# Squares on GpSimd in a fused attention and MoE kernel: 36 squares moved, 153 half-size sets, other last blocks

## The chip, the cores and the metric

The kernel runs on one core of one Trainium2 chip. The metric is the device time of one execution in microseconds. The engines are named as in the profile: PE (TensorE), DVE (VectorE), ACT (ScalarE), POOL (GpSimd) and SP (SyncE), which here only issues DMAs. POOL, SP and ACT issue DMAs.

## The reference

```python
# q, k, v: (4, 6080, 256); w_in: (256, 2048); w_out: (2048, 256)
qn = q / (norm(q, axis=1) + 1e-6)
kn = k / (norm(k, axis=1) + 1e-6)
s = kn.transpose(0, 2, 1) @ qn / tau            # (4, 256, 256)
a = exp(s - s.max(-1)); a /= a.sum(-1) + 1e-9
x = (v @ a).reshape(24320, 256)
out = gelu_tanh(x @ w_in) @ w_out
```

The norms run over the 6080 tokens, so that each batch needs the sums of squares of all columns of q and k, and the 256x256 product of k and q (the gram), before its attention matrix exists.

## The kernel before

**Folding.** The attention matrix is multiplied into w_in once per batch. This gives AW (256x2048), and the first layer is then v @ AW. The tokens of a batch are cut into blocks: five of 1024 and one of 960; in the last batch five of 1024, one of 512 and one of 448. A block's two halves, t=0 and t=1, have hc tokens each (512, 480, 256 or 224). There are 25 blocks, numbered 0 to 24.

**First layer of a block.** The 2048 hidden columns are 16 chunks of 128. A chunk and a half is done in one of two ways.
- Plainly: `mm1_one` (j, line 571) does two matmuls, `gelu_one` (J, line 583) one GELU on ACT. In the last blocks both halves can share one matmul (t=2).
- In a set ("half-size set", steps `s`): two chunks times two halves, so four plain products of two matmuls each, are made with seven matmuls of hc columns (`small`, line 639) in place of eight. The set uses sums of weights (`sums_w`, lines 605 to 611) and of v (`sums_v`, lines 618 to 622) that DVE makes. It needs two copies on ACT (cq at line 654, y5 at line 657), two additions on DVE (ap at line 659, ax at line 662) and four GELUs on ACT (lines 664 to 673). A block has at most 8 sets.

**Second layer.** Seven products with combined weights of w_out (`product`, line 750) stand for eight. DVE makes their inputs from the GELU outputs (`sums_g`, steps T, lines 723 to 733: both inputs in SBUF, up to 2048 elements a row). The results are added, transposed on DVE (`turn`, line 779) and stored in four DMAs for each half (`store`, line 795).

**Attention of the later batches.** While the blocks of one batch run, the next batch is prepared: 12 chunks of q and of k are loaded by casting DMAs that POOL issues (`load_one`, lines 254 and 256), PE adds each to the gram (`gram_row`, line 304), and `square_later` (lines 274 and 276) squares it. Step z is a square on ACT, d on DVE and e on POOL (the program before has no step e). A full chunk's square has 1024 elements a row, of bf16, in SBUF. `fold` (lines 284 to 296) adds up the squares on DVE; its first step, f.1, reads the whole chunk's squares of q and k. There are two buffers of squares. Of the 24 squares of each of the three later batches, ACT does 18 and DVE 6 (k of the even chunks).

**First batch.** Its q and k are loaded, squared and summed ahead of everything else. Then `scores` makes the attention matrix and `first_aw` the first 512 columns of AW, scaled by the row sums. `pe_vt` transposes the first block's v on PE.

**Order.** Each engine runs its instructions in the order of one long written list, `ORDER`: one word for a step, with block or batch ahead of the colon (`14:s5cq`, `b3:zq8`, `13:M3A`). Waits between engines follow from the data and the buffers. A DMA load is held back until the matmul has run that stands before it in the list (`GATE`). PSUM has eight banks, which are handed out in the order of the list.

Of the kernel before, what the change touches and what calls it, by code (L numbers as in the profile page):

```python
# [18 lines left out]
def kernel(  # L19
# [23 lines left out]
    HALF = 512  # L43
    SIZES = [[1024] * 5 + [960]] * (B - 1) + [[1024] * 5 + [512, 448]]
# [737 lines left out]
    def store(m, tj):  # L782
# [42 lines left out]
    with tc.manual_schedule():  # L825
# [49 lines left out]
        square_rows(c, 1, 0, 5, "dve")  # L875
# [3 lines left out]
        ss_rows(c, 1, range(0, 5))  # L879
# [105 lines left out]
0:j51 0:J21 0:jb1 0:s7m6 0:ja1 0:Jb1 0:s6ap 0:J51 0:J91 :pF0 0:Ja1 1:j00 0:s7ap :pS3 b0:w02 1:lt1
1:J00 0:s6m3 0:s7m3 0:s6m7 1:j50 0:s6ax 1:J50 0:j01 0:s7G1 b1:r0.0 :pS1 :pF1 0:jb0 0:j61 0:j11
0:s6G1 b1:r0.1 1:j10 0:Jb0 b1:lq1 0:s7m7 b1:lk1 b1:lq2 0:s6Gx 0:s7ax 0:s6m4 0:M1A 0:J01 1:j30 4:lv0
0:s7m4 0:J11 b1:r0.2 8:lv0 b1:lk2 0:T3a b1:lk3 3:lv0 0:M1B 0:s6Gr b1:lq4 0:J61 1:j11 1:J10 1:vs0
0:s7Gr 1:j41 :pA12 0:x1 1:J11 1:j01 1:j51 0:M2A 0:s7Gx 1:j31 1:J51 0:T1a 1:vs1 b1:r0.3 1:J30 1:s3m1
0:M2B b1:dk0 :pS2 1:J41 1:J31 1:j21 b1:zq1 1:s3m5 1:s3y5 0:T3b 1:J01 0:M5A b1:r1.0 0:T2a 1:J21  # L990
b1:r1.1 1:vs2 b1:lk5 0:T1b 1:s3cq b1:zk1 0:c11 0:M6A b1:r1.2 b1:r1.3 1:s3m2 1:s4m1 1:s4cq 0:T2b
2:lv1 b1:lq3 1:s3m6 b1:zq0 0:M5B :pS4 0:M6B 1:s4m6 0:y5 b1:r2.0 1:s4m2 1:s3ap b0:w03 1:s3G0 b1:r2.1
:pNA 0:ap 1:s4m5 1:s3m3 1:s3m7 b1:f1.1 b1:r2.2 1:s3ax b1:lk4 1:s4G0 0:M3A 1:s3G1 0:M3B b1:f0.1 2:lv0
1:s4y5 1:s5m1 1:s3Gx b1:zk3 1:s3m4 0:M7A 2:lt0 1:s4ap 1:s5cq 0:c12 1:s4m3 0:T4a 1:s4m7 1:s6m1 1:s5m2
1:s3Gr 1:s4G1 b1:r2.3 1:s4ax b1:dk2 b1:lq5 b1:f1.2 1:s5G0 1:s5m5 1:s5y5 1:s5m6 1:j20 1:s4m4 0:M7B
1:s5ap 1:s6cq 1:s4Gr 1:s4Gx 1:s6m2 1:s6G0 b1:r3.0 1:s6m5 1:s6m6 1:s5m7 1:s5m3 0:ax 1:j40 2:lt1 1:J20
1:s5G1 0:M4A 0:T4b b1:r3.1 1:J40 1:s6y5 0:M4B b1:f1.3 b1:zq2 1:s5ax 1:s7m5 1:s6ap b1:r3.2 1:s7m1
1:s5Gx b1:r3.3 1:s6m3 1:s7y5 0:c21 1:s5m4 1:s6m7 1:M1A 1:s7cq 1:s7m6 1:s5Gr b1:f2.1 1:M1B 1:T3a
1:s6ax 1:s6m4 1:s7m2 b1:r4.0 1:s6G1 b1:r4.1 1:s7ap 1:s7m3 1:T1a 1:s7m7 b1:zq3 1:s6Gx 1:x1 b1:lk6
1:s6Gr b1:lq6 1:s7ax 2:j30 1:s7G0 b1:lq7 b1:r4.2 1:s7G1 2:j11 1:s7m4 2:j01 1:T2a 1:s7Gx 1:s7Gr  # L1000
b1:f3.1 2:j20 2:vs0 2:vs1 1:M2A 2:J30 2:J20 1:T3b 2:s2m1 3:lv1 1:M2B 2:J11 2:s2m5 1:c11 2:s2cq 1:M6A
# [313 lines left out]
```

## Time and profile before

| | |
|---|---|
| median of 3 runs | 683.74 us (683.71 to 683.79) |
| the profiled execution | 683.82 us |
| its span on the core | 682.1 us, granted clock 0.998 |
| instructions | 10254 |
| HBM read and written | 78.91 MB and 36.57 MB |

A run of the kernel takes 1.7 us more than the span that the profile shows. The page has a line for each part: the busy time of each engine, the span in 40 slices, the queues, the chain of waits that ended last, and the groups of instructions. In a group's line stand the source line, the engine, the operation, output and inputs, the shape, the count, the busy time in us, the mean of one in ns, and the idle time before it with its releaser. Instructions of an engine overlap, so that the time from one start to the next is shorter than the duration of one.

### The profile page before, as it was taken

How to read it: one execution, taken by the hardware profiler on the slowest of the kernel's cores; microseconds unless marked ns; L12 is line 12 of the kernel's file. 1: busy time of each engine (PE TensorE's matmuls, PEld its weight loads, DVE VectorE, ACT ScalarE, POOL GpSimd, SP SyncE). 2: the span in 40 equal slices, each digit the busy share in tenths (PEclk: the TensorE clock that was granted, in tenths of full speed). 3: DMA queues.
4: the chain of work that ended last, by engine and by line, in shares of the span. 5: the costliest groups of instructions: out<-in, count | busy, mean ns of one | idle time of the engine just before them, and what ended most of it. 6: DMA issues, size and time to landing. Idle time of an engine off the chain costs nothing.

```text
span 682.1 us, 10254 instructions
## 1 busy us (share of the span) xinstructions
PE 660.3 (97%) x3412; PEld 333.9 (49%) x3472; DVE 630.5 (92%) x935; ACT 640.7 (94%) x1241; POOL 90.1 (13%) x165
## 2 busy tenths in 40 slices
PE   3999999999999999999999999999999999999996
PEld 2844444544445454454444544454444444444465
DVE  3579999999999999999999999999999999999996
ACT  5389999999999999999999999999999999999983
POOL 4323112111100122101020201200000000000002
PEclk9999999999999999999999999999999999999999
DMA  9997868878545896646884477668343446262453
GB/s 241 208 254 134 148 116 140 144 124 147 109 81 105 130 170 112 116 91 116 137 142 78 82 133 137 100 117 132 61 80 62 78 68 118 43 86 46 76 100 60
DMA packets 164678, 78.80 MB, mean 116 GB/s; under 512 B 148545, under 2 KB 153025, under 8 KB 163905
## 3 DMA queue, kind: packets, MB, share of 16 engines
q0 software_dynamic: 18064, 39.84, 32.9%
q1 hardware_dynamic: 145552, 37.09, 30.3%
q10 hardware_dynamic: 1008, 1.22, 0.6%
q8 instruction: 27, 0.44, 0.3%
q14 instruction: 27, 0.21, 0.1%
HBM read 78.91 MB, written 36.57 MB: 169 GB/s over the span
## 4 chain that ended last, share of the span: by engine, by line
PE 79%; ACT 14%; DMA 4%; issue 2%; POOL 0%; DVE 0%; POOLq 0%; DVEq 0%; ACTq 0%
PE u L750 20%; PE rb L639 15%; PE j L571 11%; PE p L750 10%; PE qb L639 7%; PE c L750 5%; PE G L304 4%; DMA qk<-in_k_dram 4%; PE qa L639 3%; ACT qa L654 2%; ACT g L583 2%; PE awp L512 2%; ACT g L664 2%; ACT yw L657 2%; ACT g L673 2%
## 5 line engine op out<-in xcount | busy, mean ns | idle before, releaser
L750 PEld LDWEIGHTS <-wcomb 128*128 128x128 bf16 x1400 | 136.9, 98 | 143.4
L750 PE MATMUL u<-t,wcomb 128*128 128x512 bf16 (+3 forms) x590 | 144.1, 368 | 0.4
L583 ACT ACTIVATE g<-j 128x512 bf16<-128x512 f32 (+1 forms) x196 | 119.0, 664 | 2.0 <-PE j L571 2.0
L571 PE MATMUL j<-vT,aw 128*128 128x512 bf16 (+2 forms) x410 | 114.6, 376 | 1.0 <-ACT aw L406 0.3
L659 DVE TENSOR_TENSOR qb<-rb,yw 128x512 f32<-128x512 f32 (+3 forms) x142 | 95.7, 676 | 9.2 <-PE rb L639 4.1
L639 PE MATMUL rb<-tv,sw 128*128 128x512 bf16 (+3 forms) x276 | 99.8, 372 | 0.4
L662 DVE TENSOR_TENSOR xw<-rb,yw 128x512 f32<-128x512 f32 (+3 forms) x142 | 94.5, 667 | 6.1 <-PE rb L639 3.1
L750 PE MATMUL p<-g,wcomb 128*128 128x512 bf16 (+3 forms) x393 | 96.4, 368 | 0.4
L673 ACT ACTIVATE g<-xw 128x512 bf16<-128x512 f32 (+3 forms) x142 | 94.3, 666 | 0.0
L670 ACT ACTIVATE g<-rb 128x512 bf16<-128x512 f32 (+3 forms) x142 | 88.7, 636 | 2.6 <-PE rb L639 2.5
L654 ACT ACTIVATE qa<-rb 128x512 f32<-128x512 f32 (+3 forms) x142 | 89.3, 633 | 1.4 <-PE rb L639 0.5
L667 ACT ACTIVATE g<-qb 128x512 bf16<-128x512 f32 (+3 forms) x142 | 88.7, 630 | 1.9 <-PE qb L639 1.5
L657 ACT ACTIVATE yw<-qb 128x512 f32<-128x512 f32 (+3 forms) x142 | 89.1, 632 | 1.5 <-PE qb L639 1.0
L664 ACT ACTIVATE g<-qa 128x512 bf16<-128x512 f32 (+3 forms) x142 | 88.7, 631 | 0.3 <-PE qa L639 0.2
L639 PEld LDWEIGHTS <-sw 128*128 128x128 bf16 x568 | 55.3, 98 | 58.2 <-issue 1.2
L571 PEld LDWEIGHTS <-aw 128*128 128x128 bf16 x428 | 41.6, 98 | 44.0 <-issue 1.5
L639 PEld LDWEIGHTS <-aw 128*128 128x128 bf16 x426 | 41.7, 98 | 42.4 <-issue 0.4
L317 POOL DMA_DIRECT2D vb<-in_v_dram x47 | 23.5, 501 | 276.9 <-PE qb L639 123.0
L729 DVE TENSOR_TENSOR t<-g,g 128x2048 bf16<-128x2048 bf16 (+3 forms) x50 | 58.0, 1162 | 0.3
L731 DVE TENSOR_TENSOR t<-g,g 128x2048 bf16<-128x2048 bf16 (+3 forms) x50 | 58.2, 1163 | 0.1
L723 DVE TENSOR_TENSOR g<-g 128x2048 bf16<-128x2048 bf16 (+3 forms) x50 | 58.1, 1162 | 0.2
L733 DVE TENSOR_TENSOR t<-t,g 128x2048 bf16<-128x2048 bf16 (+3 forms) x50 | 57.7, 1160 | 0.0
(133 smaller groups left out, 1002.7 us busy)
## 6 DMA issues: line engine op xcount, KB each, us to landing
out_dram<-ot SPq DMA_DIRECT2D x160, 128.0 KB, 3.0
vb<-in_v_dram POOLq DMA_DIRECT2D x37, 256.0 KB, 5.1
q<-in_q_dram POOLq DMA_DIRECT2D x33, 256.0 KB, 5.4
k<-in_k_dram POOLq DMA_DIRECT2D x33, 256.0 KB, 5.8
out_dram<-ot SPq DMA_DIRECT2D x24, 120.0 KB, 2.7
wst<-in_moe_w_out_dram POOLq DMA_DIRECT2D x2, 1024.0 KB, 11.2
qk<-in_q_dram POOLq DMA_DIRECT2D x3, 512.0 KB, 14.3
qk<-in_k_dram POOLq DMA_DIRECT2D x3, 512.0 KB, 17.0
```

Of the source, the lines that this page charges most:

```text
L571: GATE[0] = nc.tensor.matmul(hp[:, :n].rearrange("p (t x) -> p t x", t=2) if t == 2 else hp[:, :n], lhsT=AW[b][:, cc, fc * 128 : fc * 128 ...
L583: nc.scalar.activation(g[:, t, fc % 8, :hc], hp[:, :hc], AF.Gelu_apprx_tanh)
L639: GATE[0] = nc.tensor.matmul(acc[:, :hc], lhsT=lhs, rhs=rhs, start=i in (1, 5), stop=True, skip_group_check=True)
L654: nc.scalar.activation(Q0[m, p][:, :hc], RB[m, p][:, :hc], AF.Copy)
L657: nc.scalar.activation(YW[m, p][:, :hc], Q1[m, p][:, :hc], AF.Copy)
L659: nc.vector.tensor_add(Q1[m, p][:, :hc], RB[m, p][:, :hc], YW[m, p][:, :hc])
L662: nc.vector.tensor_add(XW[m, p][:, :hc], RB[m, p][:, :hc], YW.pop((m, p))[:, :hc])
L664: nc.scalar.activation(g[:, 0, e, :hc], Q0.pop((m, p))[:, :hc], AF.Gelu_apprx_tanh)
L667: nc.scalar.activation(g[:, 1, e, :hc], Q1.pop((m, p))[:, :hc], AF.Gelu_apprx_tanh)
L670: nc.scalar.activation(g[:, 0, e + 1, :hc], RB.pop((m, p))[:, :hc], AF.Gelu_apprx_tanh)
L673: nc.scalar.activation(g[:, 1, e + 1, :hc], XW.pop((m, p))[:, :hc], AF.Gelu_apprx_tanh)
L750: GATE[0] = nc.tensor.matmul(ACCS[m, acc][:, :hc], lhsT=wcomb[:, w, fc, :], rhs=x[:, fc, :], start=first and k_ == 0, stop=k_ == 3, skip_g ...
```

## The change

- All d steps and half of the z steps of the later batches become e: POOL squares k of the even chunks and q of the odd ones, 12 in a batch and 36 in all. ACT keeps the other 36.
- The list has 153 sets in place of 142. Blocks 5, 6, 7, 9, 10, 12, 13, 14, 16, 17, 18, 21 and 23 have one more, block 24 none in place of two.
- The last two blocks are of 704 and 256 tokens in place of 512 and 448. Block 23 now does its plain products by halves, block 24 all of its 16 chunks for both halves in one matmul each.
- The last block's stores are issued by ACT and SP alone. Before, its first four were issued by SP, POOL, ACT, POOL.
- First batch: half of k's squares of the last chunk's first piece goes to ACT, and two rows of them are folded on DVE, so that six matmuls sum that piece in place of eight. The first v transposes use two PSUM tiles, and DVE does both copies. The scaling of AW is done in pieces of 128 columns, two on ACT and six on DVE, and the load of the GELU table stands between them, no longer ahead.
- `ORDER` is a new list throughout.

```diff
-    SIZES = [[1024] * 5 + [960]] * (B - 1) + [[1024] * 5 + [512, 448]]
+    SIZES = [[1024] * 5 + [960]] * (B - 1) + [[1024, 1024, 1024, 1024, 1024, 704, 256]]
...
+    def fold_pair(c):
+        o = SQ0[c][:, 0:2, 256:512]
+        nc.vector.tensor_add(o, o, SQ0[c][:, 2:4, 256:512])
...
+    def pe_vt_first():
+        for cc in range(2):
+            VPS[0, 0, cc] = ps = take(("vps", 0, 0, cc), 1, [128, HALF], f"vt_ps0_0{cc}", BF16)[0]
+            for s in range(HALF // 128):
+                nc.tensor.transpose(ps[:, s * 128 : s * 128 + 128], V0[0, 0][:, s, cc * 128 : cc * 128 + 128], ident_bf)
...
-        if (m, t, cc) == (0, 0, 1):
-            nc.scalar.copy(vt(m)[:, t, cc, :], VPS[m, t][:, cc, :])
-        else:
-            nc.vector.tensor_copy(vt(m)[:, t, cc, :], VPS[m, t][:, cc, :])
+        nc.vector.tensor_copy(vt(m)[:, t, cc, :], VPS[m, t][:, cc, :])
...
-        for u in range(2):
+        for u in range(4):
             for ic in range(2):
-                nc.vector.tensor_scalar_mul(AW[b][:, ic, u * 128 : u * 128 + 128],
-                                            ps[0][ic][:, u * 128 : u * 128 + 128], rs[:, ic : ic + 1])
-        for ic in range(2):
-            nc.scalar.activation(AW[b][:, ic, 256:512], ps[1][ic], AF.Copy, scale=rs[:, ic : ic + 1])
+                o, x = AW[b][:, ic, u * 128 : u * 128 + 128], ps[u // 2][ic][:, u % 2 * 128 : u % 2 * 128 + 128]
+                if u < 2 and ic:
+                    nc.scalar.activation(o, x, AF.Copy, scale=rs[:, ic : ic + 1])
+                else:
+                    nc.vector.tensor_scalar_mul(o, x, rs[:, ic : ic + 1])
+            if u == 1:
+                nc.scalar.preload_act_table(AF.Gelu_apprx_tanh)
...
-            if m == LAST and not LAST_OUT:
-                eng = (nc.sync, nc.gpsimd, nc.scalar, nc.gpsimd)[bi]
-            elif m == LAST:
+            if m == LAST:
                 eng = (nc.scalar, nc.sync)[bi % 2]
...
-        square_rows(c, 1, 0, 5, "dve")
+        square_rows(c, 1, 0, 3, "dve")
+        square_rows(c, 1, 3, 5, "act")
+        fold_pair(c)
...
-15:s2y5 15:J10 14:T3b 15:s2m2 17:lv0 15:j11 15:j00 15:s2ap b3:r8.2 15:j20 14:T1b 15:vs2 15:s2G0
-b3:r8.3 15:J00 15:s3m1 15:J11 18:lv1 15:s2m7 14:M5A b3:f7.3 15:s2m3 14:M5B b3:r9.0 15:J20 15:s3cq
...
+13:c22 14:s3Gx 14:s5cq b3:eq7 b3:r7.0 14:s4m3 14:s5y5 b3:ek8 14:s3m4 14:s4m7 14:s5m2 14:s5m6 14:s4ax
+14:s4G1 b3:r7.1 14:s6m1 13:M4A b3:f5.4 14:s5ap 14:s5G0 b3:f7.1 14:s3Gr 14:s6cq 14:s6m5 14:s4Gx
```

More of the change, by code (lines that the diff above doesn't have):

```diff
@@ L339, with pe_vt_first_copy @@
     VPS = {}
+    def pe_vt_first():
[3 more added lines that the diff above has]
+                nc.tensor.transpose(ps[:, s * 128 : s * 128 + 128], V0[0, 0][:, s, cc * 128 : cc * 128 + 128], ident_bf)
+    def pe_vt_first_copy():
+        for cc in range(2):
+            nc.vector.tensor_copy(vt(0)[:, 0, cc, :], VPS[0, 0, cc])
+            give(("vps", 0, 0, cc))
     def pe_vt(m, t):
@@ L878 @@
         ss_rows(c, 0, range(0, 4))
-        ss_rows(c, 1, range(0, 5))
+        ss_rows(c, 1, (0, 1, 4))
         square_rows(c, 1, 5, 8, "dve")
@@ L898 @@
         warm(6)
-        pe_vt(0, 0)
+        pe_vt_first()
         scores()
-        pe_vt_copy(0, 0, 0)
-        pe_vt_copy(0, 0, 1)
-        nc.scalar.preload_act_table(AF.Gelu_apprx_tanh)
+        pe_vt_first_copy()
         first_aw()
@@ L985 @@
[L985 to L1001, printed above, removed]
@@ new lines @@
+b1:lk2 0:vs1 b0:w13 0:J81 0:vs2 0:ja0 0:s7m2 0:s6m5 0:J21 0:Ja0 0:s6m2 0:s6m6 0:j70 0:s6y5 0:J70
+0:s7m5 0:s6G0 b0:w03 0:j41 0:s7G0 b0:w12 0:j51 0:s7y5 0:s7m6 :pF0 0:j60 0:jb1 0:s6ap :pF1 0:J41
+0:s6m7 0:Jb1 0:j11 0:s7ap 1:j30 0:s6m3 0:J60 1:lt1 0:J11 0:J51 b1:r0.0 :pS3 0:s7m3 0:M1A 0:s6ax
+0:s7G1 :pA12 :pS2 0:j31 0:s6G1 1:j20 1:J20 0:M1B 0:J31 1:j10 0:s6Gx b1:r0.1 :pS1 0:T3a 1:J10 b1:lq1
+0:s6m4 0:j71 0:s7m7 1:J30 0:s7ax 1:j50 b1:lk1 1:j11 0:s6Gr 1:j41 2:lv0 0:J71 0:T1a 0:T2a 0:s7m4
+b1:lq2 1:vs0 :pS4 b1:r0.2 1:J50 1:j51 1:vs1 0:x1 b1:lq3 0:s7Gr 1:J11 1:s3m1 1:J41 4:lv0 b1:r0.3
@@ new lines @@
+2:s5m6 b1:r5.3 2:s5y5 2:s5ap 2:s6m1 2:s5G0 2:s4G1 1:M4A 2:s6cq 2:s4ax 2:s4Gx 2:s6m5 1:c22 2:s6y5
+2:s5m3 2:s5m7 1:O1 2:s6m2 2:s6m6 2:s5ax 1:M4B 2:s4m4 2:s6G0 2:s5m4 2:s5G1 b1:ek6 3:j00 b1:r6.0
+b1:r6.1 2:s7m5 2:s5Gx 2:s6ap 1:c21 2:s6m3 2:s6m7 2:s5Gr 2:s7m1 2:M1A 3:J00 2:s4Gr b1:f5.2 b1:eq7
+b1:f7.1 2:s7cq 3:j30 2:s7y5 2:s7m6 2:T3a 2:s6G1 3:J30 2:M1B 2:s6ax b1:lq8 2:s7m2 2:s6Gx 2:s6m4
+2:s7ap b1:r6.2 2:s7m7 2:s7G0 b1:lk8 2:T1a 2:s7m3 b1:r6.3 3:j11 2:s6Gr 3:j31 b1:lk11 2:s7ax b1:lq9
+3:s2m1 2:T2a b1:r7.0 2:s7G1 2:x1 b1:f5.3 2:s7m4 2:s7Gx 2:s7Gr 3:s3m1 b1:r7.1 b1:lk9 3:s3cq 3:vs0
@@ new lines @@
+4:s5m1 4:s3ax b2:lq2 4:s4m6 b1:f11.2 3:T4a 4:J20 4:s4y5 4:s4ap 3:M3B 4:s3m4 4:s5cq 4:s5m6 4:s5m2
+4:s4G0 3:c12 4:s3Gx 4:s5m5 4:s4m3 b1:f11.3 4:s4m7 b2:lk2 4:s5G0 3:M7A 4:s5y5 4:s4ax 4:s4G1 4:s3Gr
+4:s5ap 4:j11 4:s6m5 4:s6m1 4:s4Gx 4:s6cq 4:s5m3 3:M7B 4:s5m7 4:s6m6 4:s6m2 4:J11 b1:f11.4 b1:ss
+3:T4b 4:s5ax 3:ax 4:s5G1 b1:sv b1:pow 4:s6y5 4:j31 4:s5Gx 4:s4m4 4:s6ap 4:s6G0 4:s7m1 3:c22 4:s5m4
+4:J31 5:j10 4:s4Gr 4:T3a 4:s6m7 4:s5Gr 4:s7cq 3:M4A 6:lt0 3:M4B 4:s7m2 4:s7m5 b1:kf 5:J10 2:O1 b1:kr
+4:s7m6 4:s6m3 b1:krp 4:s6ax 4:T1a 4:s7G0 4:M1A 4:s7y5 b1:S0 b1:S1 4:s6Gx b1:th0 5:j31 4:s6G1 b1:th1
@@ new lines @@
+8:s4m2 8:s2Gr 8:s4y5 8:s3ax b2:f5.4 8:s4ap b2:r7.0 7:M5A 8:s3m4 8:s3G1 b2:zq6 7:M5B 8:s3Gx 8:s3Gr
+8:s4m7 7:T2b 7:y5 8:s4m3 8:s5m1 b2:r7.1 b2:lq9 b2:f6.1 b2:lk9 8:s4G1 8:s4ax 12:lv1 8:s5cq 7:M6B
+8:s4G0 8:s5m5 b2:r7.2 b2:f7.2 8:s5y5 7:ap 8:s5m6 8:s5m2 8:s6m1 8:s4m4 7:M3A b2:f7.3 8:s5ap 8:s5m3
+8:s4Gx 8:s4Gr b2:r7.3 8:s5G0 11:lv0 7:T4b 8:s7m5 8:s5G1 8:s5m7 7:M3B 8:s6cq b3:lq2 8:s6m6 8:s6m5
+b2:f7.4 b2:zq8 b2:lq10 8:s5ax b2:ek8 8:s6m2 8:s5m4 b2:r8.0 b2:lk11 7:c12 b2:r8.1 b2:eq9 8:s7m1
+8:s6y5 7:M7A 8:s5Gx 8:s5Gr 8:s6ap 8:s6m7 7:M7B 8:T3a 8:s7cq 8:s6ax 8:s7m2 8:s6G0 8:s7m6 8:s6m3
@@ new lines @@
+8:M4B b2:f11.3 9:s7y5 b2:r10.1 9:s7m6 9:s7m2 b2:r10.2 b2:r10.3 9:s7ap 9:s5Gr b2:f11.4 9:s6Gx 9:s6m4
+10:j01 b3:lk2 9:s7G0 8:c21 11:lv1 9:s7m7 9:s7ax 9:j10 b2:ss 10:s2m1 9:s7m4 b2:r11.0 9:s6Gr b2:r11.1
+10:J01 11:lt1 9:J10 10:s2cq 9:s7m3 9:T3a b2:r11.2 b2:r11.3 9:s7Gx 10:j10 b3:lk0 10:s1m1 10:vs0 b2:sv
+9:s7G1 10:s2m5 9:s7Gr 10:J10 10:vs1 10:s2m6 10:j00 9:T3b 10:s1m5 b2:pow 9:M1A 10:s2y5 b2:gc 10:s2m2
+10:s2ap 8:O0 10:J00 10:s1cq 9:M1B 10:s1m2 10:s2G0 10:vs2 10:s2m3 9:x1 10:s2m7 9:T1b 10:s3m1 10:s1y5
@@ new lines @@
+14:s7ax b3:lk11 14:s7m4 15:j30 b3:r9.1 15:J01 b3:f7.4 14:s7G1 b3:f8.1 15:s2m1 b3:r9.2 14:T2a 14:M2A
+14:s7Gx b3:ek10 15:vs0 15:s2cq 14:s7Gr b3:r9.3 b3:f9.1 15:s2m2 15:vs1 15:j11 15:J10 15:s2m6 15:J30
+15:J11 15:s2m5 b3:eq11 15:vs2 b3:f9.2 15:s2y5 15:s2G0 14:M2B 14:T3b 15:s2ap b3:r10.0 15:j20 b3:r10.1
+b3:r10.2 15:s3m1 15:s2m3 17:lt0 15:s2m7 15:s3m5 14:T1b b3:zq10 15:J20 15:s3cq 14:M6A b3:r10.3
+15:s3y5 15:s2ax 14:c11 15:s2m4 15:s3m6 b3:f9.3 15:s2G1 15:s3ap 15:s3m2 14:M5A 15:s3m7 15:s2Gx
+15:s4m1 15:s3G0 15:s3m3 b3:f9.4 15:s3ax 15:s2Gr 15:s4m5 14:T2b 15:s3G1 b3:r11.0 14:M5B 15:s4cq
@@ new lines @@
+b3:r11.1 b3:r11.2 15:s3Gx b3:r11.3 15:s4m6 14:T4a 15:s4y5 15:s3m4 14:M6B 14:y5 15:s4ap 15:s4m2
+15:s5m5 b3:gc 15:s5m1 15:s4m7 14:ap 15:s3Gr 15:s4G0 b3:zk11 13:O0 15:s6m1 14:M3A 12:O0 15:s5cq
+b3:f10.1 15:s4m3 15:s4ax 15:s4G1 14:T4b 14:M3B 15:s5y5 15:s5m6 15:s4m4 15:s6cq b3:f11.1 15:s4Gr
+15:s5ap 15:s5m2 16:lt1 14:M7A 15:s6m6 15:s5G0 15:s4Gx b3:f11.2 15:s6m5 14:c12 15:s5m7 15:s7m1
+15:s5m3 14:M7B 15:s6y5 15:s7cq 15:s5ax 15:s6m2 15:s5G1 15:s6ap 15:s5m4 15:s5Gx 14:ax 15:s7m2 15:s7m5
+15:s6m7 b3:f11.3 15:s6ax 15:s6m3 15:s7m6 14:M4A 15:s6G0 15:s7y5 15:s7G0 15:s5Gr b3:f11.4 15:s6Gx
@@ new lines @@
+14:M4B 15:s6G1 16:s1m1 15:s6m4 15:s7ap 15:s7m7 15:s7m3 15:T3a 15:s7ax b3:ss 19:lv0 16:s1cq 16:s2m1
+15:s6Gr 14:c21 15:s7G1 15:s7m4 b3:sv 16:s1m2 15:M1A 16:vs0 15:s7Gx 16:s1m5 16:s2cq 16:s2m2 16:s2m5
+16:s1G0 16:s1y5 16:vs1 16:s2y5 16:s2G0 16:s2m6 15:T1a 16:s1m6 16:s1ap 15:M1B 16:j00 16:s1m3 b3:pow
+16:s1m7 15:s7Gr 16:s2ap 16:s2m3 16:s2m7 15:x1 15:M2A b3:kf 16:s1ax 16:s1G1 16:vs2 b3:kr 16:s3m1
+16:s1Gx 16:s1m4 15:M2B 16:s1Gr 16:J00 17:lt1 16:j10 15:T3b 16:s2G1 b3:krp 16:s2ax 16:s3cq 16:s2m4
+15:T1b b3:S0 16:s2Gr 15:M5A 16:s3m2 b3:S1 16:s4m5 16:s4m1 14:O0 15:T2a 16:J10 16:s3m6 15:T2b 16:s3G0
@@ new lines @@
+23:s6m1 23:s6m5 23:s5G0 23:s4m4 23:s5m7 23:s4Gx 22:M7A 23:s6cq 23:s6m6 23:s5m3 23:s4Gr 23:s6y5
+23:s7m1 23:s5ax 23:s5Gx 23:s5G1 23:s6m2 23:s6ap 23:s6G0 23:s7cq 22:M7B 23:s3Gx 23:s5m4 23:T3a
+23:s7m5 23:s7y5 22:ax 23:s6m3 23:s5Gr 23:s7m6 23:s7ap 23:T1a 22:M3B 23:s6m7 23:s7m2 23:s7m7 23:s7m3
+23:s6ax 22:M4A 23:s2Gx 23:s6G1 23:s7ax 23:M1A 22:M4B 23:M1B 24:j22 23:s6m4 21:O1 23:s7G1 23:s7G0
+23:M5A 23:s6Gx 23:s7Gx 24:J22 23:T2a 23:x1 23:T3b 23:T1b 24:j62 22:c22 23:M5B 23:s7m4 23:M6A 24:J62
+23:T2b 23:M6B 22:c12 23:s6Gr 21:O0 24:j02 23:y5 22:c21 24:j12 23:ap 23:s7Gr 24:J02 24:ja2 24:Ja2
@@ new lines @@
+22:O1 23:T4a 23:T4b 24:j32 24:jb2 24:Jb2 23:M7A 22:O0 23:M7B 24:J12 23:M3A 23:M3B 24:j92 24:jd2
+23:ax 24:J32 23:c22 24:j52 24:j72 23:c12 24:j82 24:J92 24:Jd2 24:j42 24:je2 24:jc2 24:J52 24:J82
+24:M1A 24:jf2 24:J72 24:Je2 24:T3a 23:M2A 24:J42 24:Jc2 24:T1a 23:M4A 24:M1B 24:M5A 24:Jf2 24:T2a
+24:T3b 24:T1b 23:M4B 24:x1 24:M6A 24:T2b 24:M6B 23:c21 24:T4b 24:M5B 24:T4a 23:M2B 23:O1 24:y6
+24:M7A 23:c11 24:y5 24:M7B 24:M3A 24:M3B 24:ax 24:M2A 24:M4A 24:a12 23:O0 24:c22 24:M2B 24:c12 24:O1
+24:M4B 24:c11 24:c21 24:O0
```

529 lines of the change are left out of this document (246 added, 283 removed).

## The prediction

> **What bounds the kernel now.** I read the page first, then the busy time by stretch, then the timeline for the pace of each engine, then the groups by shape. The page's first part and its chain:
>
> ```profile
> PE 660.3 (97%) x3412; PEld 333.9 (49%) x3472; DVE 630.5 (92%) x935; ACT 640.7 (94%) x1241; POOL 90.1 (13%) x165
> ...
> PE 79%; ACT 14%; DMA 4%; issue 2%; POOL 0%; DVE 0%; POOLq 0%; DVEq 0%; ACTq 0%
> ```
>
> Three engines are nearly full and POOL is nearly empty. The chain is mostly matmuls, so a matmul saved is worth its pace as long as ACT and DVE keep up. How much DVE has left is read where the later batches' squares run (L274, L276 and the folds that read them), in three stretches; the columns are window, length, then busy PE, PEld, DVE, ACT, POOL:
>
> ```profile
> 68.00:166.00 98.00, 97.48 (x487) 48.37 (x495) 96.47 (x144) 98.00 (x186) 17.33 (x32) 1.00 0.78 136
> 200.00:310.00 110.00, 109.42 (x554) 55.10 (x564) 106.47 (x154) 109.04 (x205) 16.59 (x29) 1.00 0.67 119
> 360.00:470.00 110.00, 109.29 (x551) 54.62 (x560) 106.35 (x154) 109.64 (x207) 12.61 (x24) 1.00 0.63 109
> ```
>
> DVE idles 1.5 + 3.5 + 3.6 = 8.7 us in all of them. That is the whole cushion for anything that slows DVE there.
>
> Busy times overlap, so costs go by start to start, taken from the timeline:
>
> ```profile
> 301.57 0.38 PE L639 MATMUL qb<-tv,sw 128*128 128x512 bf16 x1
> 301.79 0.38 PE L639 MATMUL qb<-vT,sw 128*128 128x512 bf16 x1
> ```
>
> A 512-column matmul costs 0.216, 480 columns 0.202, 448 0.189, 256 0.109, 224 0.096, 128 0.056 (medians of this spacing); 352 columns are taken in proportion, 0.149. The same reading gives ACT 0.477 for a 512 GELU or copy to SBUF, 0.515 for the copy into qa, 0.520 for the GELU from SBUF, and 0.946 for a square of 1024; DVE 0.60 for ap or ax and 0.594 for a square of 1024.
>
> **The sets.** A full-size set swaps four j products (8 matmuls, 4 GELUs) for 7 matmuls, 6 ACT and 2 DVE instructions: PE -0.216, ACT +1.04, DVE +1.20 us. With the new last blocks counted by shape: j matmuls -92x0.216 -16x0.202 -24x0.189 +16x0.149 +32x0.109 = -21.8; set matmuls +70x0.216 +14x0.202 +42x0.149 -35x0.109 -14x0.096 = +19.1; two ss matmuls fewer, -0.2; the second layer's products have the same columns in all. PE: -2.9 us. On ACT the GELUs of j give -23.7 and the sets +36.6. On DVE the sets give +15.0.
>
> **The squares.**
>
> ```profile
> L274 ACT ACTIVATE sq<-q 128x1024 bf16<-128x1024 bf16 x33 | 37.5, 1144 | 0.0
> ...
> L276 DVE TENSOR_TENSOR sq<-k 128x1024 bf16<-128x1024 bf16 x18 | 12.2, 680 | 0.0
> ```
>
> ACT loses 15 squares of 1024, 3 of 768 (0.73) and 3 of 64x256 (0.31): -17.3. DVE loses 18: -10.7. So ACT ends at -4.4, DVE at +4.7 with its small edits (+0.9 for copies, scalings and the fold of the last chunk, -0.5 for the last block's sums of v). By these counts alone DVE would fit: 630.5 + 4.7 stays below PE.
>
> POOL gains the 36. No row shows a large elementwise POOL instruction. The nearest are the two that make the identity:
>
> ```profile
> 4.66 0.27 POOL masks.py:197 MEMSET ident<- 128x128 f32 x1
> 5.00 0.29 POOL masks.py:199 TENSOR_SCALAR_AFFINE_SELECT ident<-ident 128x128 f32<-128x128 f32 x1
> ```
>
> Taking 0.10 of each as fixed (the memsets of one element last 0.10 to 0.12), 128 elements cost 0.17 to 0.19, so 1024 cost 1.5 to 1.64; if nothing is fixed, 2.3. I take 1.64, the instruction that also reads, and keep 1.5 and 2.3. POOL then has 90 + 59 = 149 us of work in 682: it is not the bound. Queued behind a square on POOL are the casting loads of q, k and v. They mostly wait for a matmul anyway (vb idles 123.0 us on qb, 105.0 on rb), so up to 1.6 us of delay is hidden by that pacing; without it, one late transposed v block costs PE up to 1.6. The GpSimd Engine Reference of the Trainium skill (Performance versus the Vector engine) gives about 2.6 cycles an element at 1.2 GHz for two inputs; an estimate by it is 2.2 us a square, which would bring the forecast's sum to about 706; no row here shows it.
>
> **What a POOL square does to DVE** decides the sign. POOL read SBUF during DVE work three times here, in the pow of L439. The longest:
>
> ```profile
> 305.92 1.21 DVE L723 TENSOR_TENSOR g<-g 128x2048 bf16<-128x2048 bf16 x1
> 306.09 1.93 POOL L439 TENSOR_TENSOR rt<-sv,halves 128x4 f32<-128x4 f32 x1 [15.45 <-DVE sv L433]
> 307.05 1.22 DVE L731 TENSOR_TENSOR t<-g,g 128x2048 bf16<-128x2048 bf16 x1
> ```
>
> Four elements took 1.93, and 1.05 and 1.15 the other times. Here it began under a DVE instruction with both inputs in SBUF, which had 0.96 left to run (the next starts at 307.05); 0.96 + 0.97 = 1.93. The 1.15 began 0.16 before the end of such a one (L620), leaving 0.99; the 1.05 ran beside L662, which has one input in PSUM, and shows no wait. So POOL's reads and DVE's second SBUF input exclude each other. How long DVE waits for a POOL square is not in this trace, since four elements are read at once; its bounds are nothing and the whole square.
>
> The new order has 888 DVE steps, 398 with both inputs in SBUF (T, folds, vs, w): 0.45 of them. I assume that DVE keeps its input while such steps follow one another, so a square starts with a 0.60 us step that has at most one. The next one with two comes after one step with chance 0.45, after two with 0.25. DVE's mean wait is 0.45x(1.64-0.6) + 0.25x(1.64-1.2) = 0.58 us, or 20.8 for 36. With 1.5 it is 17.3; with 2.3, counting a third step, 1.11 each or 40.
>
> In the stretches DVE must absorb 20.8 + six of the new sets x 1.2 = 7.2, less 10.7 of squares, less 8.7 idle: 8.6 us over. DVE is then the late engine and PE waits for rb, qb and the t tiles. The break-even is 12.2/36 = 0.34 us of wait per square.
>
> **Elsewhere.** Start: PE waits 0.30 and 0.33 for the first scaled weights (L403, L406). DVE now scales u=2 and 3 behind u=0 and 1 instead of ACT behind the 1.28 us table load, which itself moves behind two ACT scalings: the first GELU starts at about 38.8 instead of 39.04. I take -0.4 (0 to -0.6). Both first vT copies on DVE (0.34 more) fit into its idle 0.38 and 0.28 there. The last chunk's split squares gain nothing, as q's last rows land only at 33.9. End: POOL's drain runs 5.02 us, from 676.25 to 681.27, and closes 0.35 after SP's; with no POOL store in the last block and 256 tokens instead of 448 in it, -0.8 (0 to -1.5). The 128-column matmuls add at most 0.01 each in weight loads. Outside the stretches the matmuls save 2.9 - 6x0.216 = 1.6, of which I count half. Sum: -2.0.
>
> Profiled execution: 683.82 + 8.6 - 2.0 = 690.4; it stands 0.08 above the median of the runs, which I drop: 690.4. With 1.5 a square the sum is 686.9, with 2.3 709.6, and some lateness is hidden by what lies ready for PE: the forecast's own range is 684 to 710.
>
> **Rivals.**
> *DVE hardly waits* (the faster side). If the squares take the input only between DVE's reads, nothing hinders PE: 683.82 - 2.9 - 0.4 - 0.8 = 679.7, about 680. For it: DVE's 2048 rows beside the pow are unchanged (1.21 and 1.22 against 1217 ns on average), and ACT is relieved too. Against it: the 0.96 us that POOL waited. It decides below 0.34 us per square.
> *First come keeps all.* A square may start at the end of any DVE step, and then the very next step with two SBUF inputs waits it out: 0.45x1.64 + 0.25x1.04 + 0.14x0.44 = 1.06 each, 38 in all, 683.82 + 38 - 12.2 - 2.0 = 707.6; 729 with 2.3 us squares. For it: the 1.93 fits a grant between two such steps. Against it: one case. This is the rule of the Trainium skill's SBUF — State Buffer (SBUF: two separate sides): the pair goes to the first that starts, for its whole instruction, and the other blocks. By that rule the trace agrees on POOL's side only.
> *The squares come too late.* The folds of b1 chunk 7 and b3 chunk 3 stand right behind their POOL square in the order, with no DVE step between; if POOL has not run ahead, each costs up to 1.64. It adds 3 us and changes no sign alone. A rest of cases ends near 684.
>
> **How the numbers follow.** Forecast 0.45 (684 to 710), first come 0.15 (705 to 729), free 0.33 (679 to 682), between 0.07. The range 679.5 to 711 leaves out most of first come and the ends. A measurement of this kernel tells 0.2% from no change: slower 0.60, same 0.07, faster 0.33.
>
> **What would show it.** Right: sq<-q and sq<-k on POOL lasting 1.5 to 2.5 us, longer than DVE's 0.68; DVE steps with two SBUF inputs lengthened or late beside them, those with PSUM not; in the stretches PE's idle time released by DVE (qb L659, t, g); after 480 us the pace of before. Wrong: DVE's mean T row still at 1.22 us and no PE waits, with the end near 680; or POOL squares above 3 us with folds waiting for POOL.

## The result, and the profile after

The changed kernel takes 715.74 us (median of 5 runs, 713.32 to 716.52) against 683.71 for the kernel before (5 runs, 683.53 to 683.79): 1.0464 times as long, interval 1.0453 to 1.0476. The forecast had the sign right and the size wrong: it said 690.4 with a range of 679.5 to 711.0.

The profiled execution of the changed kernel has a span of 714.6 us at a granted clock of 0.988. The first part of its page and its chain of waits, which answer to the two lines shown of before:

```profile
PE 667.2 (93%) x3403; PEld 332.4 (47%) x3464; DVE 666.2 (93%) x940; ACT 638.7 (89%) x1244; POOL 167.0 (23%) x202
...
PE 65%; DVE 12%; ACT 10%; issue 7%; DMA 5%; POOL 1%; DVEq 0%; POOLq 0%; ACTq 0%
```

DVE is busy 35.7 us longer with about the same work, and holds 12% of the chain, where it held none. POOL's share of the chain is 1%, and after 40 us no wait of PE, DVE or ACT in the trace ends with a POOL instruction. The busy time in the three stretches with squares, and after them (window, length, then PE, PEld, DVE, ACT, POOL, granted clock, DMA share, GB/s):

```profile
68.00:166.00 98.00, 89.55 (x430) 43.64 (x439) 92.49 (x119) 83.02 (x151) 36.19 (x38) 0.97 0.66 116
200.00:310.00 110.00, 102.00 (x494) 49.48 (x502) 106.79 (x143) 99.96 (x191) 32.72 (x34) 0.98 0.62 108
360.00:470.00 110.00, 105.82 (x522) 51.77 (x531) 108.00 (x151) 105.26 (x203) 32.23 (x35) 1.00 0.67 116
480.00:700.00 220.00, 218.73 (x1047) 104.35 (x1067) 212.38 (x305) 213.19 (x442) 7.40 (x13) 0.99 0.42 74
```

PE was busy 97.48 of the first 98 us before and is now busy 89.55; behind the squares, after 480 us, it is full again. DVE issues 119 instructions in the first window in place of 144 and is still busy for 92.49 us: its instructions last longer. Which ones is read from the groups by shape:

```profile
L748 DVE TENSOR_TENSOR t<-t,g 128x2048 bf16<-128x2048 bf16 x40 | 56.6, 1420 | 0.0
L744 DVE TENSOR_TENSOR t<-g,g 128x2048 bf16<-128x2048 bf16 x40 | 54.1, 1354 | 0.1
...
L674 DVE TENSOR_TENSOR qb<-rb,yw 128x512 f32<-128x512 f32 x128 | 87.7, 691 | 6.8 <-ACT yw L672 3.6 <-PE rb L654 2.5 <-PE qa L654 0.3
...
L280 POOL TENSOR_TENSOR sq<-k 128x1024 bf16<-128x1024 bf16 x18 | 38.0, 2111 | 21.0 <-ACT qa L669 10.0 <-ACT g L688 4.3 <-ACT yw L672 3.9
L280 POOL TENSOR_TENSOR sq<-q 128x1024 bf16<-128x1024 bf16 x15 | 31.3, 2088 | 32.7 <-DVE a L288 23.6 <-ACT g L685 6.7 <-DVE a L292 2.2
```

The same two T steps before:

```profile
L733 DVE TENSOR_TENSOR t<-t,g 128x2048 bf16<-128x2048 bf16 x40 | 48.6, 1214 | 0.0
L729 DVE TENSOR_TENSOR t<-g,g 128x2048 bf16<-128x2048 bf16 x40 | 48.5, 1215 | 0.2
```

Both have both inputs in SBUF, and they went from 1214 and 1215 ns to 1420 and 1354. The ap step, with one input in PSUM, stays at 691 (693 before). Added up over the trace, 23 DVE steps are longer than their shape's median, by 31.4 us together, 0.87 for each of the 36 squares; all have both inputs in SBUF. This count, made the same way for the kernels below, misses a step whose shape occurs only once: L718 at 62.51 us lasts 2.94, against 1.22 in the kernel whose POOL only writes. With it there are 24 steps and 33.2 us. The median POOL square of 1024 lasts 1.91 us; the mean of 2.1 holds longer ones, up to 2.9.

The timeline at the second longest stop of PE:

```profile
100.72 0.53 POOL L258 DMA_DIRECT2D k<-in_k_dram  x1 [1.39 <-PE rb L654]
...
101.01 5.10 DVE L744 TENSOR_TENSOR t<-g,g 128x2048 bf16<-128x2048 bf16 x1
...
101.27 1.91 POOL L280 TENSOR_TENSOR sq<-k 128x1024 bf16<-128x1024 bf16 x1
...
103.13 1.90 POOL L280 TENSOR_TENSOR sq<-q 128x1024 bf16<-128x1024 bf16 x1
...
106.17 1.02 PE L765 MATMUL u<-t,wcomb 128*128 128x512 bf16 x4 [3.58 <-DVE t L744]
...
107.37 0.58 PE L654 MATMUL rb<-tv,aw 128*128 128x512 bf16 x1 [0.18 <-DVE xw L677]
```

A T step of 1.22 us lasts 5.10. It ends 1.08 us behind the end of the second POOL square (103.13 + 1.90 = 105.03), so that most of its work was done only when both were over. PE stood for 3.58 us for its tile, and then its 512-column matmul shows 0.58 us instead of 0.38. The busy time in three windows there shows why:

```profile
102.60:106.10 3.50, 0.00 (x0) 0.00 (x0) 3.50 (x2) 0.89 (x2) 2.42 (x2) 1.00 0.48 88
107.10:110.50 3.40, 3.22 (x11) 1.43 (x10) 2.15 (x5) 2.10 (x4) 0.00 (x0) 0.50 0.00 0
110.50:114.00 3.50, 3.45 (x17) 1.55 (x16) 3.37 (x4) 3.42 (x7) 0.00 (x0) 1.00 0.09 21
```

Behind the stop the granted clock is 0.50 for a while: 11 matmuls where the next window has 17. The trace has four such pieces of 3.41 us after 40 us (from 69.6, 107.1, 277.8 and 479.2), behind stops of 4.04, 3.58, 2.56 and 2.92 us. If PE is full in them, they cost 4 x 3.41 x 0.5 = 6.8 us. All gaps of PE after 40 us come to 29.6 us, where before had 3.7; but some 60 gaps of about 0.05 us in each are matmuls whose records are missing (3403 matmuls stand beside 3464 weight loads). Stops of over 0.1 us are 24, with 26.4 us, against 0.6 us before, and DVE steps end 25.2 of the 26.4. Where stops are summed below, these are meant.

### The profile page after: what moved, and what is told of

Its sections match the earlier page's. It is cut to its first block, busy times and chain, and to the rows that moved or that the text cites. A ratio compares the mean times of both kernels' runs of the same rounds, so it can differ in the third digit from the quotient of the medians.

```text
span 714.6 us, 10336 instructions
## 1 busy us (share of the span) xinstructions
PE 667.2 (93%) x3403; PEld 332.4 (47%) x3464; DVE 666.2 (93%) x940; ACT 638.7 (89%) x1244; POOL 167.0 (23%) x202
## 4 chain that ended last, share of the span: by engine, by line
PE 65%; DVE 12%; ACT 10%; issue 7%; DMA 5%; POOL 1%; DVEq 0%; POOLq 0%; ACTq 0%
PE u L765 17%; PE rb L654 14%; PE p L765 9%; PE qb L654 7%; PE j L586 6%; PE c L765 4%; DMA qk<-in_k_dram 4%; PE qa L654 3%; PE G L308 3%; DVE t L748 2%; ACT qa L669 2%; DVE xw L677 2%; DVE qb L674 2%; ACT g L688 1%; ACT g L685 1%
## 5 line engine op out<-in xcount | busy, mean ns | idle before, releaser
L654 PE MATMUL rb<-tv,sw 128*128 128x512 bf16 (+2 forms) x293 | 108.5, 377 | 6.4 <-DVE qb L674 6.0
L688 ACT ACTIVATE g<-xw 128x512 bf16<-128x512 f32 (+2 forms) x153 | 103.1, 681 | 9.3 <-DVE xw L677 9.3
L674 DVE TENSOR_TENSOR qb<-rb,yw 128x512 f32<-128x512 f32 (+2 forms) x153 | 103.3, 681 | 7.8 <-ACT yw L672 3.6
L677 DVE TENSOR_TENSOR xw<-rb,yw 128x512 f32<-128x512 f32 (+2 forms) x153 | 102.2, 672 | 4.9 <-PE rb L654 2.5
L682 ACT ACTIVATE g<-qb 128x512 bf16<-128x512 f32 (+2 forms) x153 | 98.0, 647 | 9.1 <-PE qb L654 9.0
L669 ACT ACTIVATE qa<-rb 128x512 f32<-128x512 f32 (+2 forms) x153 | 97.2, 646 | 5.7 <-DVE ot L794 3.2
L672 ACT ACTIVATE yw<-qb 128x512 f32<-128x512 f32 (+2 forms) x153 | 97.3, 646 | 4.3 <-PE qb L654 4.1
L679 ACT ACTIVATE g<-qa 128x512 bf16<-128x512 f32 (+2 forms) x153 | 97.8, 653 | 2.7 <-PE qa L654 2.3
L598 ACT ACTIVATE g<-j 128x512 bf16<-128x512 f32 (+2 forms) x156 | 92.9, 640 | 8.0 <-PE j L586 7.0
L685 ACT ACTIVATE g<-rb 128x512 bf16<-128x512 f32 (+2 forms) x153 | 98.4, 650 | 0.7 <-PE rb L654 0.4
```

The lines of the kernel that those rows point to most:

```text
L598: nc.scalar.activation(g[:, t, fc % 8, :hc], hp[:, :hc], AF.Gelu_apprx_tanh)
L654: GATE[0] = nc.tensor.matmul(acc[:, :hc], lhsT=lhs, rhs=rhs, start=i in (1, 5), stop=True, skip_group_check=True)
L669: nc.scalar.activation(Q0[m, p][:, :hc], RB[m, p][:, :hc], AF.Copy)
L672: nc.scalar.activation(YW[m, p][:, :hc], Q1[m, p][:, :hc], AF.Copy)
L674: nc.vector.tensor_add(Q1[m, p][:, :hc], RB[m, p][:, :hc], YW[m, p][:, :hc])
L677: nc.vector.tensor_add(XW[m, p][:, :hc], RB[m, p][:, :hc], YW.pop((m, p))[:, :hc])
```

## The experiments

Measured beside these kernels, the kernel before took 683.56 us (GpSimd only writes, squares on GpSimd alone, no GpSimd squares, half on GpSimd), 683.73 us (one input, four pieces, fewer sets, start and end alone) and 683.79 us (one at a time, in pairs).

**GpSimd only writes.** In `square_later`, two memsets stand in for each POOL square:

```diff
-                (nc.vector if on == "d" else nc.gpsimd).tensor_mul(o, t[:np_, r, :], t[:np_, r, :])
+                for _ in range(2):
+                    nc.gpsimd.memset(o, 0.01)
```

> The changed kernel with each POOL square replaced by two POOL memsets of the same tile region, so that POOL writes and does not read SBUF; the later batches' sums of squares are left out (a constant stands in their place). Theory (the shared read): DVE steps keep their lengths, 1.21 us for a T row, and the time is 679 to 684, which is also the price of all other parts of the change. Rival (POOL itself, as a late engine or by its queue of loads): 710 or more, as POOL is as busy as with the squares.

Measured: 680.44 us, 0.9952 of before (0.9938 to 0.9967). Its page's first part, and its group of memsets:

```profile
PE 660.9 (97%) x3464; PEld 331.0 (49%) x3464; DVE 633.5 (93%) x940; ACT 635.3 (94%) x1244; POOL 156.4 (23%) x241
```
```profile
L281 POOL MEMSET sq<- 128x1024 bf16 x66 | 62.5, 956 | 39.3 <-DVE a L289 27.7 <-ACT g L686 5.1 <-ACT qa L670 4.6
```

POOL is busy for about as long as with the squares (156.4 against 167.0) and hands over at the same places; no DVE step is lengthened, and PE stands for 0.6 us in all after 40 us. So POOL's lateness, its queue of loads and the new list cost nothing. The 35.3 us to the changed kernel come from POOL reading SBUF. A memset also doesn't wait for its chunk's load, as a square does; but in the changed kernel the squares waited for a load only once after 40 us, for 2.8 us. The rest of the change is worth -3.1 us.

**Squares on GpSimd alone.** The kernel before, with the same 36 squares turned into e steps in its list (all d, and half of the z):

```diff
-... b1:dk0 ... b1:zq1 ...
+... b1:ek0 ... b1:eq1 ...
```

> The kernel before with the same 36 squares moved to POOL and nothing else. Theory: the wait alone, 0.87 us a square on DVE as in the changed kernel, less what 10.7 us of freed DVE time hides, and some half-clock stretches: 703 to 716. Rival (new list and sets are the loss): 680 to 685, as ACT and DVE are both relieved.

Measured: 715.71 us, 1.0463 (1.0444 to 1.0483), and 27 DVE steps lengthened by 38.9 us. One part of the change makes the whole of its loss. What sets and ends gain when POOL only writes is not seen beside the waits.

**One input.** Each POOL square becomes an instruction that reads the tile once; a constant takes the place of the squares:

```diff
-                (nc.vector if on == "d" else nc.gpsimd).tensor_mul(o, t[:np_, r, :], t[:np_, r, :])
+                nc.gpsimd.tensor_scalar(o, t[:np_, r, :], 0.0, 0.01, op0=ALU.mult, op1=ALU.add)
```

> The changed kernel with each GpSimd square replaced by one GpSimd instruction that reads the same tile once (times 0, plus 0.01; a constant stands in place of the squares). Theory A (any GpSimd read of SBUF keeps VectorE's two-input steps waiting): steps with both inputs in SBUF are lengthened by up to the length of the GpSimd instruction, and the time lies between 690 and 715 us, by how long that instruction is beside 1.91 us. Theory B (only a GpSimd instruction with two SBUF inputs does it): no VectorE step is lengthened and the time is that with GpSimd only writing, 679-683 us.

Measured: 692.76 us, 1.0135 (1.0121 to 1.0149). The instruction lasts 1.07 us (median), 19 DVE steps are lengthened by 13.5 us, at most 2.2, and PE stands for 9.0 us after 40 us. One read is enough; theory B falls. What is shorter costs less: 12.3 us above the writing kernel, for 36 x 1.07 = 38 us of POOL reading, against 35.3 for 36 x 1.91 = 69.

**Four pieces.** Each full square is issued as four instructions of 256 elements:

```diff
+                if on == "d" or np_ < 128:
...
+                else:
+                    for i in range(n):
+                        nc.gpsimd.tensor_mul(o[:, i, :], t[:, i, :], t[:, i, :])
```

> The changed kernel with each GpSimd square issued as four instructions of 256 elements instead of one of 1024. Theory A (VectorE is kept out of SBUF only while one GpSimd instruction reads, and gets in at its end): a VectorE step waits at most about 0.5 us at a time, TensorE's idle stretches of 2.5 us and more and the half-clock stretches behind them go, and the time falls to 690-705 us. Theory B (GpSimd keeps VectorE out until its own queue has nothing ready, as the step did that lasted across both squares from 101.27 to 105.03 us): the waits stay as long as the four together or longer, and the time is 712-720 us.

Measured: 702.33 us, 1.0270 (1.0254 to 1.0285): the time that theory A gave, by a mechanism that is only half A's. Of 41 lengthened steps, together 23.5 us, most are late by 0.3 to 0.5 us, about one piece's 0.61. But four wait longer, through runs of pieces, one of them for 4.7 us; behind it PE stops for 4.42 us and the clock is halved for 6.83, so that not all long stops went:

```profile
97.30 5.93 DVE L748 TENSOR_TENSOR t<-g,g 128x2048 bf16<-128x2048 bf16 x1
97.55 2.32 POOL L284 TENSOR_TENSOR sq<-k 128x256 bf16<-128x256 bf16 x4
99.84 2.31 POOL L284 TENSOR_TENSOR sq<-q 128x256 bf16<-128x256 bf16 x4
```

Eight pieces on end run at 0.57 us each, and DVE gets in behind the last. At other places the two engines take turns. Which of the two happens is not settled.

**One at a time, or in pairs.** Of the 36 POOL squares 18 stay; two memsets stand in for each of the others. In the first kernel the q squares stay, in the second the neighbouring pairs of chunks 0 and 1, 4 and 5, 8 and 9 (there the condition is `(c // 2) % 2 == 0` in place of `which == 0`):

```diff
-                (nc.vector if on == "d" else nc.gpsimd).tensor_mul(o, t[:np_, r, :], t[:np_, r, :])
+                if on == "d" or which == 0:
+                    (nc.vector if on == "d" else nc.gpsimd).tensor_mul(o, t[:np_, r, :], t[:np_, r, :])
+                else:
+                    for _ in range(2):
+                        nc.gpsimd.memset(o, 0.01)
```

> The changed kernel with 18 of the 36 GpSimd squares left (the q ones, which then run one at a time) and two memsets in place of each of the others, whose values are a constant. Theory A (a wait of up to 1.9 us is partly taken up by work in hand, and it is the waits of two squares on end that reach TensorE and halve its clock): under 690 us. Theory B (every square costs VectorE the 0.87 us of the changed kernel's mean and nearly all of it reaches the end): 18 x 0.87 x 0.92 = 14.4 us above the kernel with GpSimd only writing, 694-698 us.

> The changed kernel with 18 of the 36 GpSimd squares left in neighbouring pairs (chunks 0, 1, 4, 5, 8 and 9) and two memsets in place of each of the others, whose values are a constant. Theory A (it is the waits of two squares on end that reach TensorE and halve its clock): 696-702 us, at least 5 us above the kernel with the 18 one at a time. Theory B (every square costs the same wherever it stands): 694-698 us, within 2 us of it.

Measured: one at a time 689.94 us, 1.0092 (1.0076 to 1.0109); in pairs 702.27 us, 1.0278 (1.0263 to 1.0293). The two theories differ in the distance between the kernels, at least 5 us or within 2; it is 12.3, which is theory A's. Its two times were met only at their edges (under 690, and 696 to 702). Above the writing kernel that is 9.5/18 = 0.53 us a square against 21.8/18 = 1.21. The timeline of the pairs at their longest wait:

```profile
283.95 1.91 POOL L281 TENSOR_TENSOR sq<-k 128x1024 bf16<-128x1024 bf16 x1
284.01 5.92 DVE L750 TENSOR_TENSOR t<-g,g 128x2048 bf16<-128x2048 bf16 x1
...
285.79 0.59 POOL L258 DMA_DIRECT2D k<-in_k_dram  x1
...
286.94 1.90 POOL L281 TENSOR_TENSOR sq<-q 128x1024 bf16<-128x1024 bf16 x1
```

The step waits through both squares and the DMAs issued between them. In pairs, DVE's lengthening is 19.7 us, at most 4.7, PE stands for 17.6 us after 40 us, and the clock is halved twice. One at a time it is 12.2 us, at most 1.7, PE stands for 7.5, and the clock is never halved behind a stop. The squares that stay are not the same ones in the two kernels, so a part of the difference may be their places in the list; that was not tested.

**No GpSimd squares.** The changed list with its e squares given back, those of q to ACT and those of k to DVE:

```diff
-            if on == "z":
+            if on == "z" or (on == "e" and which == 0):
...
-                (nc.vector if on == "d" else nc.gpsimd).tensor_mul(o, t[:np_, r, :], t[:np_, r, :])
+                nc.vector.tensor_mul(o, t[:np_, r, :], t[:np_, r, :])
```

> The changed kernel with its 36 POOL squares given back: q of the odd chunks to ACT, k of the even ones to DVE; list, sets, last blocks, start and end as changed. Theory (a POOL square keeps DVE's steps with two SBUF inputs waiting, 31.4 us of lengthened DVE steps in the changed kernel's trace, and PE idles and then runs 3.4 us at half clock): no DVE step lengthened, PE idle after 40 us back from 29.6 to under 6 us, time 680 to 688, the upper end because DVE then carries 646 us. Rival (the new list and the 11 more sets are the loss): 705 or more.

Measured: 702.14 us, 1.0264 (1.0247 to 1.0281). This is neither number: no DVE step is lengthened, as the theory has it, but 18 squares on each engine cost 21.7 us over the kernel in which they take neither's time. PE stands for 12.7 us, where under 6 were expected, and the clock is halved for 6.83 us behind a stop of 2.56.

**Half on GpSimd.** Only q's squares stay on POOL, k's go to DVE:

```diff
-                (nc.vector if on == "d" else nc.gpsimd).tensor_mul(o, t[:np_, r, :], t[:np_, r, :])
+                (nc.vector if on == "d" or which == 1 else nc.gpsimd).tensor_mul(o, t[:np_, r, :], t[:np_, r, :])
```

> The changed kernel with only q of the odd chunks on POOL (18 squares), k of the even chunks on DVE, so that POOL no longer runs two squares back to back. Theory: 18 single waits of at most 1.9 us, 0.6 us on average, and DVE carries 10.7 us more: 688 to 698, PE idles of under 2 us and so no half clock. Rival (order and sets): 710 to 716.

Measured: 706.25 us, 1.0331 (1.0315 to 1.0346), with 14 DVE steps lengthened by 15.8 us. PE's stops reach 2.23 us, and the clock is halved once, behind one of 2.07, which the theory had excluded. The result lies between the two, and the kernel that runs 18 squares one at a time shows why: with the same squares on POOL and none of the others on DVE it takes 689.94. So DVE's 18 squares, 12.3 us of work in the kernel above, cost 16.3 us at these places of the list, where DVE also waits longer for POOL (15.8 us against 12.2).

**Fewer sets.** To see whether those 21.7 us are too much work, the kernel without GpSimd squares gets 12 of its sets back as plain products (141 sets, one fewer in each of 12 blocks; block 5's words):

```diff
-5:s2m1 5:s2cq 5:s2m5 5:s2m2 5:s2m6 5:s2y5 5:s2ap 5:s2m3 5:s2G0 5:s2m7 5:s2G1 5:s2ax 5:s2m4 5:s2Gx 5:s2Gr
+5:j40 5:J40 5:j41 5:j50 5:j51 5:J41 5:J50 5:J51
```

> The changed kernel with the 36 squares back on ScalarE and VectorE, and 12 of its sets turned back into plain products (141 sets). Theory A (the 702 us of the changed kernel without GpSimd squares are VectorE and ScalarE being asked for more than TensorE leaves time for in 60-480 us): 12 sets fewer take 14 us off VectorE and 12 us off ScalarE and put 2.6 us on TensorE, and the time is 682-690 us. Theory B (the shape of the list, with squares back at places where the list has no room, makes the stalls): the time stays at 696-702 us.

Measured: 702.31 us, 1.0276 (1.0262 to 1.0290); theory A falls. Its stretches:

```profile
68.00:166.00 98.00, 93.93 (x459) 45.50 (x468) 91.19 (x132) 93.85 (x172) 16.27 (x31) 1.00 0.75 131
200.00:310.00 110.00, 104.16 (x512) 50.79 (x521) 100.47 (x143) 104.61 (x196) 14.21 (x27) 1.00 0.66 114
360.00:470.00 110.00, 106.74 (x526) 52.17 (x536) 102.16 (x152) 106.41 (x200) 15.49 (x30) 1.00 0.64 111
```

No engine is full: PE, DVE and ACT all idle 3 to 10 us in each stretch. They wait for each other in turn. One case is plain. In the kernel with all sets and no GpSimd squares, a square on DVE at 241.77 us waits 2.98 us for the load of its chunk, ahead of the xw step, and PE stops for 2.56; here the same square, at 242.20, waits 2.13, and PE stops for 2.55. For most of the rest it is inferred from this, and not shown, that the squares stand at places of the list that were made for an engine with nothing else to do.

**Start and end alone.** The kernel before with the new start (scaling of AW, table load, first transposes, fold of the last chunk's squares) and its last block's stores on ACT and SP, all as in the change; the core of it:

```diff
+                if u < 2 and ic:
+                    nc.scalar.activation(o, x, AF.Copy, scale=rs[:, ic : ic + 1])
+                else:
+                    nc.vector.tensor_scalar_mul(o, x, rs[:, ic : ic + 1])
...
-            if m == LAST and not LAST_OUT:
-                eng = (nc.sync, nc.gpsimd, nc.scalar, nc.gpsimd)[bi]
```

> The kernel before with only the change's start (first batch's scaling shared differently, the last chunk's squares folded together) and its last block's stores shared over two queues. Theory A (the small edits at the ends are worth what the prediction put on them): 0.4-0.8 us off the kernel before, 682.9-683.3 us. Theory B (the ends are hidden anyway and the 3.1 us that the changed kernel with GpSimd only writing gains come from the sets alone): within 0.2 us of the kernel before.

Measured: 681.43 us, 0.9966 (0.9953 to 0.9978), more than either theory gave, and faster than both kernels. The lines of the timeline that show the start, the last group of gram matmuls of before and its first GELUs, and then the same of this kernel:

```profile
34.12 0.60 PE L206 MATMUL G<-qk 128*128 128x256 bf16 x4
...
39.04 1.19 ACT L583 ACTIVATE g<-j 128x512 bf16<-128x512 f32 x2
```
```profile
33.68 0.60 PE L210 MATMUL G<-qk 128*128 128x256 bf16 x4
...
38.42 1.08 ACT L598 ACTIVATE g<-j 128x512 bf16<-128x512 f32 x2
```

The last gram group starts 0.44 us earlier, and the first GELU 0.62. The 0.44 are not the fold's: the group starts 0.25 us behind the landing of q's last load, at 33.87 before and 33.44 here, and the kernel with the squares on GpSimd alone, whose start is the old one, has that load at 33.47 and the group at 33.73. From the end of that group to the tenth GELU it is 13.09 us before, 13.11 in that kernel and 12.33 here, so the new scaling is worth 0.8 us. The blocks run 0.9 to 1.2 us ahead from there, 1.2 at their end; the span is 2.4 shorter (679.64 against 682.05), and the other 1.2 come at the stores and POOL's drain.

## Why the forecast was wrong

**POOL's square.** Taken as 1.64 (1.5 to 2.3), its median is 1.91. The bounds held. The GPSIMD Engine Reference of the Trainium skill (Performance versus the Vector engine) has about 2.6 cycles an element at 1.2 GHz, which gave the estimate of 2.2 us; the trace has 1.91, between the two.

**DVE's mean wait.** The step said 0.58 us a square, the trace has 0.87. Most of the difference is the duration: with 1.91 in the same formula it is 0.45x(1.91-0.6) + 0.25x(1.91-1.2) + 0.14x(1.91-1.8) = 0.78. "First come" would give 0.45x1.91 + 0.25x1.31 + 0.14x0.71 = 1.29, too much. The formula's picture was still wrong. It had DVE keep its input and POOL slip in; the trace has few steps that wait long, up to 3.9 us, and a step that waits through two squares. This term gives 31.4 us for 20.8, so 10.6 of the miss (12.4 with L718's step).

**The cushion** is the step that failed most. The sum let DVE's idle 8.7 us and its freed 10.7, less 7.2 for new sets, take up 12.2 us of the waits, so that 8.6 would show. The changed kernel lies 35.3 us above the one whose POOL only writes and which has the same list and the same cushion, for 31.4 us of waits (33.2 with L718's). Nothing was taken up on balance. PE's stops grew by 25.8 us against that kernel, and the halved clock added about 6.8: 32.6, against 35.9 in the spans (714.6 - 678.7). The sum is rough: a matmul is recorded for 0.38 us and paced at 0.216, so that each of the 24 stops can be up to 0.16 us longer than recorded, 3.9 in all, and the spans lie within that. Two things made the cushion worthless. It was an average over 100 us, while the waits come in pieces of 2 to 4 us, and a few steps later PE has nothing ready: waits of 12.2 us in pieces up to 1.7 reach the end as 9.5, and waits of 19.7 in pieces up to 4.7 as 21.8. And idle time of DVE in a full list is not stock: taking sets back freed 12.4 us of DVE's busy time and 7.5 of ACT's (644.7 to 632.3 and 652.2 to 644.7) and gained nothing.

**The halved clock** was no term of the sum. It is about 6.8 us of the result.

**The rest.** -4.1 was put on sets, start and end if nothing hindered PE (the rival of 679.7); the kernel with POOL only writing gives 680.44. In its parts, start and end were too small: -0.4 and -0.8, together 1.2, where they make 2.3 in the kernel before. By the traces the scaling makes 0.8 of it and the end 1.2; 0.4 is the load that landed earlier in the profiled execution. "The last chunk's split squares gain nothing" held: the last gram group waits for that load in either kernel. If start and end are worth as much in the new list, the sets, put at -2.9, show about 1 us of it: 681.43 - 680.44. Where the rest went wasn't traced.

**The rivals.** The fast one named the right price for the change without POOL's reads, but the reads do hold DVE. "First come keeps all" was nearer in time (707.6), and its range of 705 to 729 holds the result, but in part by luck: it counted 38 us of waits and leaned on the same cushion. It is the rule of the Trainium skill's SBUF — State Buffer (SBUF: two separate sides): the first to start keeps the ports for its whole instruction. The trace agrees that the other then waits it out, as the T step at 101.01 did for 3.9 us; but a step held through two squares, the second of which starts 2.1 us behind it, goes beyond the instruction that the rule names, and by the records this step even started 0.26 us ahead of the first. The third rival, squares that come too late, falls by the kernel that only writes. The signs named for "right" all came: 1.5 to 2.5 us a square, PSUM steps unchanged, PE released by DVE, and the old pace after 480 us.

## What to carry to other kernels

An engine with idle time is no free place for work if its reads lock out an engine that feeds the bound: price the work by what it makes the other wait, and test that price with the same instructions made to write only. Idle time summed over a long stretch covers many small delays and no large one; ask how long the longest single wait is, and what the bound has ready for that long. Where locking work must stay, keep it one instruction at a time: 18 squares cost 9.5 us apart and 21.8 in pairs.

## What the runs showed of the hardware

- A DVE step with both inputs in SBUF can wait through two POOL instructions on end (101.01), through two with 1.1 us of DMA issue between them (284.01), and through eight short ones (97.30), though its own start is recorded up to 0.26 us ahead of the first. One step, at 65.37 in the changed kernel, is recorded 1.08 us ahead of its square, with two DMA issues of POOL between, and still waits that square out; PE's longest stop, 4.04 us, hangs on it. The records' starts are rough, so that who came first is not shown. Nor is it settled when a step waits through more than one: the step that waits through two at 284.01 (in pairs) waits in the changed kernel, at 293.25, for the first alone, beside the same POOL instructions.
- POOL's writes alone hold up nothing here: 78 memsets, 0.956 us for 1024 elements, and no DVE step longer.
- The granted clock halves for 3.41 us, or twice that: behind a stop of PE of 2.56 us in the changed kernel, and behind one of 1.89 in the kernel that reads once. Another stop of 2.55 us (the kernel with fewer sets) and one of 2.21 (the changed kernel) left it at 1.00. The traces tell these apart. From the clock's first rise to its last change, the times between two changes are whole multiples of 3.413 us in all twelve (in the changed kernel 15, 1, 10, 1, 49, 1, 58, 1 and 67 of them), so that it changes only on a fixed grid. By these traces it counts how long PE stands within one piece of this grid: between 40 us and the last 30 us the clock fell twelve times, behind pieces with 1.89 to 3.37 us without a matmul, and the longest without a fall is 1.91. The stop of 2.55 was cut by the grid into 0.88 and 1.67, that of 2.21 into two parts of which the longer had 1.59. TensorE: Matmul & The Clock Gate of the Trainium skill (What's actually happening) has a free-running window of 3.4 us, which the grid of 3.413 bears out.
